# ScalarE's copy of turned tile 3 placed between the two halves of tile 1's k eviction

## The chip, the cores and the metric

The kernel runs on 1 core of a Trainium2 chip. The metric is the device time of one execution in microseconds, the median of several runs. The clock granted to TensorE was 1.00 in the profiled execution.

## The reference

Input x is 2048 x 640 in bf16. Out comes x, plus a linear attention block on the layer-normed x, plus a routed block of which eight rows are changed.

```python
xn = _layernorm(x, axis=-1)
return x + _A_ref(xn, A_wqkv, A_wo) + _B_ref(xn, B_w_r, B_w_gate, B_w_up, B_w_down)
# A: 32 heads of 20; phi = where(t > 0, t + 1, exp(t)) + 1e-6
#    kv = sum_s phi(k) v ; z = sum_s phi(k) ; o = phi(q) kv / (phi(q) z) ; o @ wo
# B: r = xn @ w_r ; the 8 rows with the largest r go through silu(x w_gate) * (x w_up) @ w_down,
#    scaled by sigmoid(r), and are added to xn at their places
```

## The kernel before

The 2048 rows are 16 tiles of 128 rows. The order on each engine is the order in which the program is written (`tc.manual_schedule()`), and each engine works through its own queue in that order; waits between engines are set by the data and by the buffers.

For each tile t the first phase does this. VectorE takes the statistics of x (`stat`, L176 and L178). The reciprocal root comes from ScalarE for tiles 0 to 3 and 8 (`root_act`, L182 and L183) and from GpSimd for the others (`root_pool`, L187 and L188). VectorE then writes the normed tile `xn` (`norm_dve`, L197). The tile must be turned, with its 640 features on the partitions, to be a weight for k = xn @ wk. Tiles 0 to 3 are turned on TensorE (`tr_pe`, L216: five 128 x 128 pieces, three into PSUM bank 7 and two into bank 6) and copied to `xnT` by `tr_ev`: the three pieces of bank 7 by ScalarE (L222) and the two of bank 6 by VectorE (L227). Tiles 4 to 15 are turned by a DMA on the SP queue (`tr_dma`, L230). On the same queue the load of x tiles 10 to 15 (`load_x`, L99) stands behind the transposes of tiles 4, 5 and 6, and weight loads stand between the later transposes.

k of a tile is two halves of 320 columns (`k_half`, L238, five matmuls each), in two PSUM banks: 2 and 3 for tile 1, 4 and 5 for tile 2, 0 and 1 for the others. The second half of each tile but tile 0 has a 321st column, the router's r. ScalarE evicts each half with an Exp and a Relu (`k_act`, L255 and L256), and copies the router column out of the second half (L258). VectorE joins both halves into phi(k) in one instruction (`k_phi`, L262). phi(k) and `xn` give the sum over rows that later makes kv (`g1`, L269, in banks 2 to 6). q is computed transposed, 20 pieces of 128 x 512 (`q_mm` L277, `q_act` L286 and L287, `q_phi` L293), the first three in the stretch around the change.

Around the change the program order, L413 to L447, is: first half of tile 0's eviction, statistics of tile 3, k of tile 1 with the turning of tile 2 between its halves, `tr_ev(2)`, the root of tile 3, the second half of tile 0's eviction, the router column of tile 0, **tile 1's eviction (both halves)**, statistics of tile 4 and norm of tile 3, k of tile 2 with the turning of tile 3 between its halves, **`tr_ev(3)`**, tile 2's eviction, and k of tile 3, which reads turned tile 3. The second phase, after tile 15's k, finishes the sums, the routed rows, the rest of q, and the output (`o_mm`, L833; `o_out`, L842).

Of the kernel before, what the change touches and what calls it, by code (L numbers as in the profile page):

```python
# [38 lines left out]
def kernel(  # L39
# [116 lines left out]
    def router_0():  # L156
        for kc in range(KC):
            PE.matmul(
                ps[:, 6, 400:401], lhsT=xnT[:, kc, 0:P], rhs=wk[:, kc, D : D + 1],
                start=(kc == 0), stop=(kc == KC - 1),  # L160
            )
# [13 lines left out]
    def stat(t, b):  # L175
        V.bn_stats(out=stats[:, t, b, :], in_=x_sb[:, t, b * HW : (b + 1) * HW])  # L176
        if b:
            V.bn_aggr(out=mv[:, t, :], in_=stats[:, t, :, :])  # L178
# [41 lines left out]
    def tr_ev(t, other=A):  # L220
        dst = xnT[:, :, t * P : (t + 1) * P]
        A.copy(dst[:, 0:3, :], psb[:, 7, 0 : 3 * P].rearrange("p (k f) -> p k f", k=3))  # L222
        src = psb[:, 6, 0 : 2 * P].rearrange("p (k f) -> p k f", k=2)
        if other is A:
            A.copy(dst[:, 3:, :], src)
        else:
            V.tensor_copy(dst[:, 3:, :], src)  # L227
# [6 lines left out]
    def k_half(t, b):  # L234
        b0 = K_BANK.get(t, 0)
        n = HW + (b if t else 0)
        for kc in range(KC):
            PE.matmul(  # L238
                ps[:, b0 + b, 0:n],
                lhsT=xnT[:, kc, t * P : (t + 1) * P],  # L240
                rhs=wk[:, kc, b * HW : b * HW + n],
                start=(kc == 0), stop=(kc == KC - 1),
            )
# [3 lines left out]
    def k_act(t, halves=(0, 1)):  # L247
        b0 = K_BANK.get(t, 0)
        if t not in kev:
            e = evk.tile([P, 2, HW], BF16, tag="ek", name=f"ek{t}")  # L250
            r = evk.tile([P, 2, HW], BF16, tag="rk", name=f"rk{t}")
            kev[t] = e, r
        e, r = kev[t]
        for b in halves:
            A.activation(e[:, b, :], ps[:, b0 + b, 0:HW], AF.Exp)  # L255
            A.activation(r[:, b, :], ps[:, b0 + b, 0:HW], AF.Relu)  # L256
            if b and t:
                A.copy(r_all[:, t : t + 1], ps[:, b0 + 1, HW : HW + 1])  # L258
# [163 lines left out]
    root_act(3)  # L422
    k_act(0, (1,))
    router_0()
    k_act(1)
    stat(4, 0)
    norm_dve(3)
    stat(4, 1)
# [2 lines left out]
    tr_pe(3)  # L431
    k_half(2, 1)
    tr_ev(3, V)
    k_act(2)
    stat(5, 0)
    k_phi(0)
# [499 lines left out]
```

## Time and profile before

| | us |
|---|---|
| median of 3 runs | 111.95 (111.92 to 112.37) |
| the profiled execution's own time | 112.4 |
| its span, first to last instruction | 110.7 |
| busy: TensorE, VectorE, ScalarE, GpSimd | 105.0, 83.2, 62.0, 41.0 |
| TensorE's wait for turned tile 3 at 13.14 | 0.78 |
| TensorE's wait for turned tile 15 at 50.37 | 0.16 |

Times in the trace are microseconds from the span's start. A row of a timeline has the start, the duration, the engine (PE is TensorE, PEld its weight loads, DVE VectorE, ACT ScalarE, POOL GpSimd, SPq the queue of DMAs that SyncE issues), the line of the kernel, the operation, the output and the inputs, and in brackets how long the engine stood idle before it and what released it. The chain of waits follows the last instruction back to what it hung on, and is printed in order of time. The table of stretches has, for each stretch, its length, the busy time and number of instructions of TensorE, its weight loads, VectorE, ScalarE and GpSimd, the granted clock, the busy share of the DMA engines and GB/s. Ends of matmuls are modelled, so a block's listed end may lie a little past the start of the next one.

### The profile page before, as it was taken

The page shows a single profiled execution, that of the slowest core. Times are in us where ns is not written, and L with a number is a line of the kernel's source. Part 1 is how long each engine was busy: PE and PEld are TensorE (multiplying, and loading weights), DVE is VectorE, ACT ScalarE, POOL GpSimd, SP SyncE. Part 2 cuts the span into 40 slices and gives each one's busy share as a digit, 9 for nine tenths or more (in the row PEclk, how much of TensorE's full clock was granted, in tenths as well). Part 3 has the DMA queues.
Part 4 walks back from the last instruction along what each step waited for, and adds up shares of the span by engine and source line. Part 5 has one row for each costly group of instructions (what it writes and reads, how often), then busy time and mean ns, then how long its engine had stood idle before and what let it go on. Part 6 is the DMA issues. An engine that isn't in the chain of part 4 may idle for free.

```text
span 110.7 us, 2559 instructions
## 1 busy us (share of the span) xinstructions
PE 105.0 (95%) x926; PEld 61.4 (55%) x926; DVE 83.2 (75%) x186; ACT 62.0 (56%) x160; POOL 41.0 (37%) x88
## 2 busy tenths in 40 slices
PE   5989799999999999999999999999999999999990
PEld 2256454665555565554436879534447766666660
DVE  1789987877999998753919964698599664788880
ACT  1449996799776666665019445588985735000000
POOL 6930273120067755899999430000000410000310
PEclk9999999999999999999999999999999999999999
DMA  3999237791758799989999979729928195783333
GB/s 84 325 341 331 103 65 63 131 328 20 197 138 160 194 182 220 199 189 287 259 248 401 391 260 266 219 68 319 356 79 177 32 330 188 169 322 118 114 121 118
DMA packets 28551, 22.46 MB, mean 203 GB/s; under 512 B 11634, under 2 KB 27258, under 8 KB 28538
## 3 DMA queue, kind: packets, MB, share of 16 engines
q1 hardware_dynamic: 23664, 18.44, 60.8%
q10 hardware_dynamic: 4810, 3.85, 11.1%
q8 instruction: 7, 0.11, 0.5%
q14 instruction: 6, 0.05, 0.2%
q0 software_dynamic: 64, 0.01, 0.1%
HBM read 14.79 MB, written 5.43 MB: 183 GB/s over the span
## 4 chain that ended last, share of the span: by engine, by line
PE 54%; DVE 22%; DMA 11%; POOL 5%; ACT 3%; issue 2%; SPq 0%; POOLq 0%; ACTq 0%
PE ps L833 19%; PE ps L277 12%; DMA x_sb<-in_A_x_dram 8%; DVE pk L262 6%; DVE stats L176 5%; DVE xn L197 5%; PE ps L269 5%; PE ps L531 4%; DVE pqT L293 3%; DMA xnT<-xn 3%; PE ps L238 3%; POOL rs L188 2%; DVE mv L178 2%; PE ps L685 2%; PE ps L768 2%
## 5 line engine op out<-in xcount | busy, mean ns | idle before, releaser
L238 PE MATMUL ps<-wk,xnT 128*128 128x320 bf16 (+1 forms) x160 | 25.0, 300 | 1.1 <-ACT xnT L222 1.0
L277 PE MATMUL ps<-xnT,wq 128*128 128x512 bf16 x100 | 23.7, 379 | 0.0
L833 PE MATMUL ps<-late,pqT 128*128 128x320 bf16 x150 | 21.8, 300 | 0.1
L238 PEld LDWEIGHTS <-xnT 128*128 128x128 bf16 x160 | 15.1, 97 | 9.7 <-ACT xnT L222 1.6
L269 PE MATMUL ps<-pk,xn 128*128 128x512 bf16 x80 | 19.6, 379 | 0.0
L255 ACT ACTIVATE ek<-ps 128x320 bf16<-128x320 f32 x32 | 14.6, 457 | 8.4 <-PE ps L238 8.4
L833 PEld LDWEIGHTS <-pqT 128*128 128x128 bf16 x150 | 13.9, 98 | 7.2 <-DVE pqT L640 1.9
L176 DVE BATCH_NORM_STATS2 stats<-x_sb 128x6 f32<-128x320 bf16 x32 | 14.7, 474 | 3.3 <-DMA x_sb<-in_A_x_dram 3.3
L286 ACT ACTIVATE eq<-ps 128x512 bf16<-128x512 f32 x20 | 12.0, 598 | 8.9 <-PE ps L277 8.9
L293 DVE SCALAR_TENSOR_TENSOR pqT<-eq,rq 128x512 bf16<-128x512 bf16 x20 | 14.2, 710 | 3.3 <-ACT rq L287 3.1
L842 DVE TENSOR_TENSOR o<-ps,x_sb 128x640 bf16<-128x640 f32 x15 | 12.4, 824 | 5.4 <-PE ps L833 3.0
L262 DVE SCALAR_TENSOR_TENSOR pk<-ek,rk 128x640 bf16<-128x640 bf16 x16 | 13.1, 823 | 3.2 <-ACT rk L256 3.2
L277 PEld LDWEIGHTS <-wq 128*128 128x128 bf16 x100 | 9.4, 98 | 10.6 <-issue 0.7
L256 ACT ACTIVATE rk<-ps 128x320 bf16<-128x320 f32 x32 | 14.6, 457 | 0.0
L208 POOL TENSOR_SCALAR x_sb<-x_sb,rs,nm 128x640 bf16<-128x640 bf16 x13 | 13.9, 1079 | 0.6
L269 PEld LDWEIGHTS <-xn 128*128 128x128 bf16 x80 | 7.6, 98 | 8.1
L287 ACT ACTIVATE rq<-ps 128x512 bf16<-128x512 f32 x20 | 11.9, 593 | 0.0
L187 POOL TENSOR_SCALAR t<-mv 128x1 bf16<-128x1 f32 x11 | 3.6, 326 | 22.2 <-DVE mv L178 22.0
L197 DVE TENSOR_SCALAR xn<-x_sb,mv,rs 128x640 bf16<-128x640 bf16 x16 | 8.3, 516 | 3.1 <-POOL rs L188 2.4
L188 POOL TENSOR_TENSOR rs<-t,mhalf 128x1 f32<-128x1 bf16 x11 | 9.4, 858 | 0.9
L884 POOL DMA_INDIRECT s_dram<-y,idx_i x1 | 1.6, 1594 | 20.4 <-ACT y L880 20.4
L869 ACT CAST o<-ps 128x160 bf16<-128x160 f32 x1 | 0.3, 293 | 13.9 <-PE ps L859 13.9
(129 smaller groups left out, 104.2 us busy)
## 6 DMA issues: line engine op xcount, KB each, us to landing
wg<-in_B_w_gate_dram SPq DMA_DIRECT2D x5, 384.0 KB, 3.4
wu<-in_B_w_up_dram SPq DMA_DIRECT2D x5, 384.0 KB, 8.9
wd<-in_B_w_down_dram SPq DMA_DIRECT2D x4, 480.0 KB, 11.0
spare<-rd SPq DMA_DIRECT2D x3, 640.0 KB, 5.5
rd<-rden ACTq DMA_DIRECT2D x1, 1280.0 KB, 7.1
out_dram<-o SPq DMA_DIRECT2D x8, 160.0 KB, 2.3
out_dram<-o ACTq DMA_DIRECT2D x7, 160.0 KB, 2.6
wo<-in_A_wo_dram SPq DMA_DIRECT2D x2, 500.0 KB, 8.2
```

What stands on the lines that cost most here:

```text
L176: V.bn_stats(out=stats[:, t, b, :], in_=x_sb[:, t, b * HW : (b + 1) * HW])
L197: V.tensor_scalar(out=xn[:, t, :], in0=x_sb[:, t, :], scalar1=mv[:, t, 0:1], scalar2=rs[:, t : t + 1], op0=ALU.subtract, op1=ALU.mult,)
L208: G.tensor_scalar(out=x_sb[:, t, :], in0=x_sb[:, t, :], scalar1=rs1[:, sl], scalar2=nm[:, sl], op0=ALU.mult, op1=ALU.add,)
L238: PE.matmul(ps[:, b0 + b, 0:n], lhsT=xnT[:, kc, t * P : (t + 1) * P], rhs=wk[:, kc, b * HW : b * HW + n], start=(kc == 0), stop=(kc == KC ...
L255: A.activation(e[:, b, :], ps[:, b0 + b, 0:HW], AF.Exp)
L256: A.activation(r[:, b, :], ps[:, b0 + b, 0:HW], AF.Relu)
L262: V.scalar_tensor_tensor(out=pk[:, t, :].rearrange("p (b f) -> p b f", b=2), in0=e[:], scalar=1.0, in1=r[:], op0=ALU.min, op1=ALU.add,)
L269: PE.matmul(ps[:, 2 + c, :], lhsT=xn[:, t, c * P : (c + 1) * P], rhs=pk[:, t, 0:512], start=(t == 0), stop=(t == T - 1),)
L277: PE.matmul(ps[:, bank, :], lhsT=wq[:, kc, m * P : (m + 1) * P], rhs=xnT[:, kc, tb * 512 : (tb + 1) * 512], start=(kc == 0), stop=(kc == K ...
L293: V.scalar_tensor_tensor(out=pqT[:, m, tb * 512 : (tb + 1) * 512], in0=e[:], scalar=1.0, in1=r[:], op0=ALU.min, op1=ALU.add,)
L833: PE.matmul(ps[:, b0 + b, 0:HW], lhsT=pqT[:, kc, t * P : (t + 1) * P], rhs=Ms[:, kc, b * HW : (b + 1) * HW], start=(kc == 0), stop=(kc == ...
L842: V.tensor_tensor(out=o_t[:], in0=ps[:, b0 : b0 + 2, 0:HW], in1=x_sb[:, t, :].rearrange("p (b f) -> p b f", b=2), op=ALU.add,)
```

## The change

`k_act` takes the halves that it is to evict. Before, tile 1's eviction is one call with both. Now the first half stays where it was, and the second half stands behind `tr_ev(3)`.

```diff
     k_act(0, (1,))
     router_0()
-    k_act(1)
+    k_act(1, (0,))
     stat(4, 0)
     norm_dve(3)
     stat(4, 1)
...
     tr_pe(3)
     k_half(2, 1)
     tr_ev(3, V)
+    k_act(1, (1,))
     k_act(2)
     stat(5, 0)
     k_phi(0)
```

The one place where instructions move is ScalarE's queue between tile 0's eviction and tile 2's. `ek1` and `rk1` are the Exp and the Relu of tile 1, `ek2` and `rk2` those of tile 2, `ps` is PSUM, `xnT` the turned tiles; rows of before alone have a -, rows of the changed kernel alone a +.

```order
 L255 ACTIVATE ek1_259<-ps_72 128x320
 L256 ACTIVATE rk1_260<-ps_72 128x320
-L255 ACTIVATE ek1_259<-ps_72 128x320 [waits PE_49]
+L222 COPY xnT_80<-ps_72 128x3x128 [waits PE_49]
+L255 ACTIVATE ek1_259<-ps_72 128x320
 L256 ACTIVATE rk1_260<-ps_72 128x320
 L258 CAST r_all_129<-ps_72 128x1
-L222 COPY xnT_80<-ps_72 128x3x128 [waits PE_49]
 L255 ACTIVATE ek2_289<-ps_72 128x320
 L256 ACTIVATE rk2_290<-ps_72 128x320
```

The copy has moved ahead of three instructions. It keeps its wait for TensorE, which now stands ahead of the second Exp, and since the transposes of tile 3 lie behind the second half of tile 1's k on TensorE, the Exp needs no wait of its own any more. All other rows of ScalarE stand as before, and so do all rows of TensorE, VectorE, GpSimd and SP.

The SP queue's rows of which the prediction speaks are these, the same in both kernels: the transposes of tiles 4, 5 and 6, the load of x tiles 10 to 15, and the transposes of tiles 7 and 8.

```order
L230 DMA_TRANSPOSE xnT<-xn 128x5x128 [waits DMAHW4_49,DVE_49]
L230 DMA_TRANSPOSE xnT<-xn 128x5x128 [waits DMAHW5_49,DVE_49]
L230 DMA_TRANSPOSE xnT<-xn 128x5x128 [waits DMAHW6_49,DVE_49]
L99 DMA x_sb<-in_A_x_dram 128x6x640 [waits DMAHW7_49]
L230 DMA_TRANSPOSE xnT<-xn 128x5x128 [waits DMAHW0_49,DVE_49]
L230 DMA_TRANSPOSE xnT<-xn 128x5x128 [waits DMAHW1_49,DVE_49]
```

Nothing moved here: the load stands behind three transposes, each of which waits for VectorE's norm of its tile.

## The prediction

> **What bounds the kernel now.** First the head of the page, to see which engine is full.
>
> ```profile
> span 110.7 us, 2559 instructions
> PE 105.0 (95%) x926; PEld 61.4 (55%) x926; DVE 83.2 (75%) x186; ACT 62.0 (56%) x160; POOL 41.0 (37%) x88
> ```
>
> TensorE is busy for 95% of the span, so time can only come out of its 5.7 us of idle time or out of its work, and the change leaves the work alone. The question is which of its waits the change touches, and whether the end follows. Second, therefore, TensorE's timeline around the moved copy and at tile 15's k (start, duration, then idle time and its releaser in brackets).
>
> ```profile
> 11.23 0.45 PE L216 MATMUL ps<-ident,xn 128*128 128x128 bf16 x5
> 11.52 0.85 PE L238 MATMUL ps<-wk,xnT 128*128 128x321 bf16 x5
> 13.14 1.54 PE L238 MATMUL ps<-wk,xnT 128*128 128x320 bf16 x10 [0.78 <-ACT xnT L222]
> ...
> 15.60 1.24 PE L269 MATMUL ps<-pk,xn 128*128 128x512 bf16 x5
> ```
> ```profile
> 42.72 1.53 PE L238 MATMUL ps<-wk,xnT 128*128 128x320 bf16 x10
> ...
> 47.60 1.53 PE L238 MATMUL ps<-wk,xnT 128*128 128x320 bf16 x10
> ...
> 50.37 1.54 PE L238 MATMUL ps<-wk,xnT 128*128 128x320 bf16 x10 [0.16 <-DMA xnT<-xn]
> ```
>
> TensorE turns tile 3 from 11.23 (L216), does tile 2's second k half until 12.37, then stands 0.78 us until ScalarE has copied turned tile 3 (L222). From there it shows no idle note in its rows up to tile 15's k at 50.37, where it stands 0.16 us for a **DMA**: turned tile 15. So two paths meet at 50.37. TensorE's own would have been there at 50.37 - 0.16 = 50.21; the transposed tile landed later.
>
> Third, the chain of waits, which shows what that tile hung on.
>
> ```profile
> 16.80 0.45 DVE xn L197
> ...
> 18.98 0.40 SPq L230
> ...
> 19.43 6.15 DMA x_sb<-in_A_x_dram
> ...
> 46.55 0.45 DVE xn L197
> ...
> 47.02 3.30 DMA xnT<-xn
> 50.33 0.05 issue
> 50.37 1.54 PE ps L238 x10
> ```
>
> This chain passes the tiles' statistics, shifts and roots on VectorE and GpSimd, the load of x tiles 10 to 15 (from 19.43, for 6.15 us), VectorE again, and the transpose of tile 15 (47.02 to 50.33). I call it **the tile chain**. The 0.78 us wait of TensorE isn't on it. Fourth, the busy time of one stretch shows that the tile chain has no slack of its own behind the load.
>
> ```profile
> 25.60:43.30 17.70, 17.70 (x104) 9.92 (x103) 17.53 (x41) 12.64 (x37) 8.32 (x14) 1.00 0.70 163
> ```
>
> The columns are TensorE, its weight loads, VectorE, ScalarE and GpSimd. From the load's end to 43.3 VectorE is busy for 17.53 of 17.70 us and ScalarE for 12.64: VectorE works off a backlog here and waits for no ScalarE result. TensorE is without a gap there as well, which is why the two paths run side by side up to 50.
>
> **The change, part by part.** No instruction is added or taken away. On ScalarE one copy changes places with the Exp, the Relu and the one-column cast of tile 1's second half:
>
> ```profile
> 11.55 0.45 ACT L256 ACTIVATE rk<-ps 128x320 bf16<-128x320 f32 x1
> 11.87 0.46 ACT L255 ACTIVATE ek<-ps 128x320 bf16<-128x320 f32 x1
> 12.19 0.47 ACT L256 ACTIVATE rk<-ps 128x320 bf16<-128x320 f32 x1
> 12.50 0.21 ACT L258 CAST r_all<-ps 128x1 bf16<-128x1 f32 x1
> 12.54 0.55 ACT L222 COPY xnT<-ps 128x384 bf16<-128x384 bf16 x1
> 12.91 0.52 ACT L255 ACTIVATE ek<-ps 128x320 bf16<-128x320 f32 x1
> ```
>
> 1. *The copy.* ScalarE starts one of these every 0.32 us and the cast takes 12.54 - 12.50 = 0.04. In the place of the second Exp, at 11.87, the copy starts 12.54 - 11.87 = **0.67 us earlier**. Its own wait, for the transposes of tile 3, doesn't hold it: all five are over at 11.23 + 0.45 = 11.68. It ends at 11.87 + 0.55 = 12.42, so TensorE, free at 11.52 + 0.85 = 12.37, starts tile 3's k at about 12.47 and not at 13.14. The idle 0.78 falls to about 0.11. VectorE's part of tile 3 doesn't take over as the late one: its copy (L227, in the rows below) is over at 12.01.
>
> The Trainium skill, "ScalarE: Activation LUTs", section "What ACT_TABLE_LOAD costs", gives an Exp of 320 columns 186 + 0.833 x 320 = 453 ns with an overlap of about 93, thus one start each 0.36 us. The durations agree (0.44 to 0.47), the distance of the starts does not (0.32). By the page the copy would gain 2 x 0.36 + 0.04 = 0.76 and not 0.67; the measurement decides.
>
> 2. *What is moved back.* Exp, Relu and cast of tile 1's second half start one copy slot later, 12.91 - 12.54 = 0.37 us, and their output is there at about 12.19 + 0.47 + 0.37 = 13.03. Its reader is VectorE's k of tile 1 (L262, below), at 15.52: 2.5 us of room. From 12.91 on ScalarE's order is as before, and so are its times, as it is back to back there. TensorE's g1 of tile 0, now at 15.60 - 0.67 = 14.93, overwrites the banks from which k of tiles 1 and 2 and the router column are read; the last of these reads, below, ends at 14.23 + 0.31 = 14.54. Cost: nothing, with 0.39 us in hand.
>
> ```profile
> 14.23 0.31 ACT L164 CAST r_all<-ps 128x1 bf16<-128x1 f32 x1
> ```
> ```profile
> 11.73 0.28 DVE L227 COPY xnT<-ps 128x256 bf16<-128x256 bf16 x1
> ...
> 15.52 0.82 DVE L262 SCALAR_TENSOR_TENSOR pk<-ek,rk 128x640 bf16<-128x640 bf16 x1
> ```
>
> 3. *What TensorE does with 0.67 us.* It is earlier by that much at every later tile, until a transposed tile isn't there. Tiles 12 and 14, at 42.72 and 47.60 before, would start at 42.05 and 46.93. Their transposes left at 38.87 and 44.33:
>
> ```profile
> 38.87 1.21 SPq L230 DMA_TRANSPOSE xnT<-xn  x1
> ...
> 44.33 1.21 SPq L230 DMA_TRANSPOSE xnT<-xn  x1
> ```
> ```profile
> DMA to landing us min/median/max: 2.6/2.9/3.6
> ```
>
> With the median of 2.9 us they land at 41.8 and 47.2. By tile 14 TensorE has caught up with the tile chain, and at tile 15 it stands until 50.33 whatever it did before. Wait there: 0.16 + 0.67 = 0.83 us, less what it waited at the tiles just before.
>
> 4. *Does the tile chain itself move?* No DMA, no VectorE and no GpSimd instruction changes place, and the transposes' queue is not touched. VectorE's reads of ScalarE's results before 47 have room (2.5 us for the nearest, in step 2). I take 0, bounded by 0 and, above, by the copies' overlap: VectorE's L227 now runs beside ScalarE's copy out of the neighbouring bank, at most some 0.01 us by the 0.29 that such a copy took at 9.96, beside one:
>
> ```profile
> 9.96 0.29 DVE L227 COPY xnT<-ps 128x256 bf16<-128x256 bf16 x1
> ```
>
> **Sum** against the profiled execution's 112.4 us (1.7 more than its span): 0.67 gained at 12.4, 0.67 given back by 50.33, nothing from there on, 112.4 again. The runs' median is 111.95, the profiled execution 0.45 above it, which I put to the execution and not to the kernel; the forecast is that median, with at most a crumb off: **111.9 us**.
>
> **Rivals.** *Faster: the tile chain is earlier in other executions.* Only 0.12 us (50.33 - 50.21) make it the later path in this one. It has one odd row, the second transpose issued, which took 2.43 us where the others took 1.2:
>
> ```profile
> 15.63 2.43 SPq L230 DMA_TRANSPOSE xnT<-xn  x1
> ```
>
> The third and the load of x stand behind it. Had it taken 1.2, the third could have left when its tile was ready (16.80 + 0.45 = 17.25) and the load at about 18.5 and not 19.43, and VectorE's stall behind that load is 1.45 us long:
>
> ```profile
> 25.60 0.49 DVE L176 BATCH_NORM_STATS2 stats<-x_sb 128x6 f32<-128x320 bf16 x1 [1.45 <-DMA x_sb<-in_A_x_dram]
> ```
>
> The tile chain would come 0.9 earlier, TensorE would be the bound at 50.21, and the change would give all of its 0.67: 111.95 - 0.67 = 111.3. For it speak that row, tile 15's 3.30 us against the median of 2.9, and the 0.45 us between the runs. Against it: whatever shifts the first loads shifts both paths alike. A part of it (0.1 to 0.5 us) is quite possible and stays within 0.5%. Chance of over 0.56 us: 0.22.
>
> *Slower: one more slow issue on the transposes' queue.* Place: the SP queue at 17 to 19.4, where the load of x tiles 10 to 15 stands behind three transposes. If TensorE's and ScalarE's shifted work makes the third take 2.43 as well, the load leaves 1.2 us later, VectorE's stall grows from 1.45 to 2.65, tile 15 lands at 51.5, and the end is 1.2 later: 113.1. It decides from a load 0.56 us late. Against it: only one of twelve issues was slow, and nothing names the change as its cause. Chance 0.07.
>
> *The change doesn't do what it says: the copy stands in the way.* If the transposes ended later than 11.87 by some w, ScalarE would stand for w with tile 1's second half behind the copy. That ScalarE does stand so is seen at 6.11:
>
> ```profile
> 6.11 0.48 ACT L222 COPY xnT<-ps 128x384 bf16<-128x384 bf16 x1 [1.20 <-PE ps L216]
> ```
>
> With w = 0.67 TensorE gains nothing (112.0, within 0.5%); VectorE, and the time, would suffer only from w = 2.5, the room of step 2, and be 0.56 slower from w = 3.1 (112.5 and up). The rows put the transposes 0.19 ahead. The Trainium skill, "PSUM — Partial Sum Buffer", section "Engine vs sequencer instructions", says that ScalarE's queue is strictly first in, first out, so nothing could pass the waiting copy; the row at 6.11 agrees. Chance of a slower time this way: 0.01.
>
> **How the numbers follow.** Forecast, absorbed wholly or but for under 0.56 us: 0.70. Faster: 0.22. Slower: 0.07 + 0.01 = 0.08. The bound of 0.5% is about what a measurement of this kernel can tell from no change. The range reaches down to the full gain with a little scatter, 111.2, and up to the highest run of before, 112.4, which leaves out the slow issue.
>
> **What would show it.** Right: tile 3's copy at about 11.9, the k behind it at about 12.5 with 0.1 idle, the load of x at 19.4 as before, and an idle of up to 0.8 us put down to the transposed tiles (L238 from 46 to 50.4), tile 15's k again near 50.4. Wrong: tile 15's k at 49.7 with little idle ahead of it (the faster rival), the load after 20 (the slower one), or ScalarE idle ahead of the copy (the third). My step that can fail first is step 4, that the tile chain in the timed runs stands where this one execution shows it.

## The result and the profile after

The changed kernel takes **111.45 us** (median of 10 runs, 111.06 to 112.45), the kernel before 111.99 us (10 runs, 111.92 to 112.52) in the same comparison: a ratio of 0.995, 95% interval 0.9926 to 0.9974, so 0.54 us or 0.5% faster. The forecast was 111.9 in a range of 111.2 to 112.4. The changed kernel was compared a second time, with other runs: 111.95 us (12 runs, 111.24 to 112.28) against 112.07 (23 runs), ratio 0.9985, interval 0.9965 to 1.0006. The single runs of the first comparison spread over 1.4 us, and the experiments below ask what moves them. Only one execution of each kernel and comparison has a trace; what the others did is not seen in rows. All profiles below show a granted clock of 0.998 to 1.00.

The head of the changed kernel's page (its profiled execution took 111.98 us):

```profile
span 110.3 us, 2550 instructions
PE 104.1 (94%) x917; PEld 61.0 (55%) x926; DVE 84.1 (76%) x186; ACT 62.0 (56%) x160; POOL 41.3 (37%) x88
```

The span is 0.4 us shorter. The nine instructions fewer are nine missing matmul records, so TensorE's busy time can't be compared with that of before. ScalarE's timeline of the changed kernel at the place of the change:

```profile
11.72 0.45 ACT L256 ACTIVATE rk<-ps 128x320 bf16<-128x320 f32 x1
12.03 0.50 ACT L222 COPY xnT<-ps 128x384 bf16<-128x384 bf16 x1
12.39 0.48 ACT L255 ACTIVATE ek<-ps 128x320 bf16<-128x320 f32 x1
12.72 0.48 ACT L256 ACTIVATE rk<-ps 128x320 bf16<-128x320 f32 x1
13.04 0.22 ACT L258 CAST r_all<-ps 128x1 bf16<-128x1 f32 x1
13.08 0.52 ACT L255 ACTIVATE ek<-ps 128x320 bf16<-128x320 f32 x1
...
16.26 0.82 ACT L287 ACTIVATE rq<-ps 128x512 bf16<-128x512 f32 x1
```

And TensorE's, from the turning of tile 3 on:

```profile
11.39 0.45 PE L216 MATMUL ps<-ident,xn 128*128 128x128 bf16 x5
11.68 2.45 PE L238 MATMUL ps<-wk,xnT 128*128 128x321 bf16 x15
14.18 1.02 PE L277 MATMUL ps<-xnT,wq 128*128 128x512 bf16 x4
15.05 1.24 PE L269 MATMUL ps<-pk,xn 128*128 128x512 bf16 x5
16.12 2.32 PE L277 MATMUL ps<-xnT,wq 128*128 128x512 bf16 x10
...
38.64 1.24 PE L269 MATMUL ps<-pk,xn 128*128 128x512 bf16 x5
39.90 1.54 PE L238 MATMUL ps<-wk,xnT 128*128 128x320 bf16 x10
...
46.16 1.24 PE L269 MATMUL ps<-pk,xn 128*128 128x512 bf16 x5
47.29 1.54 PE L238 MATMUL ps<-wk,xnT 128*128 128x320 bf16 x10
48.67 1.24 PE L269 MATMUL ps<-pk,xn 128*128 128x512 bf16 x5
49.95 1.54 PE L238 MATMUL ps<-wk,xnT 128*128 128x320 bf16 x10
```

This execution runs 0.16 us late already at the turning of tile 3 (11.39 and not 11.23), so distances count and not clock times. The copy starts 12.03 - 11.39 = 0.64 after the turning, where it was 12.54 - 11.23 = 1.31: 0.67 us earlier, to the digit of the forecast. The k of tile 2's second half and of tile 3 are now one row of 15 with no idle time noted. A stretch that begins at 12.55 shows where tile 3's k starts in it:

```profile
12.59 1.54 PE L238 MATMUL ps<-wk,xnT 128*128 128x320 bf16 x10
```

That is 12.59 - 11.39 = 1.20 us after the turning (1.19 to 1.20 in all profiles of the changed order), where it was 13.14 - 11.23 = 1.91. **TensorE gains 0.71 to 0.72 us at the copy.** It still waits for the copy: ten matmuls of this block take 1.38 us to the next block's start (47.29 to 48.67), five 0.69, so that tile 2's half is done at 11.68 + 0.69 = 12.37, and tile 3's k stands another 0.22 us. By the same reckoning it stood 13.14 - (11.52 + 0.69) = 0.93 us before.

It then gives some back. A g1 block of five matmuls takes 1.07 to 1.08 us to the next block's start where nothing is late (here 15.05 to 16.12). From 38.64 the next k should start at 39.72 and starts at 39.90; from 46.16 at 47.24, and starts at 47.29; from 48.67 at 49.75, and starts at 49.95. That is 0.18 + 0.05 + 0.20 = 0.43 us. Modelled ends hide such waits: the profile notes no idle time there. In the profile of before it noted 0.16 us at tile 15, and the g1 block ahead of it is this:

```profile
48.97 1.24 PE L269 MATMUL ps<-pk,xn 128*128 128x512 bf16 x5
```

By the distance (48.97 + 1.08 = 50.05, start at 50.37) 0.32 us were lost there. The waits of the weight loads tell what was late, in the changed kernel from 10 to 52 us (waiting engine and line, releaser, us in total, times, longest):

```profile
DVE stats L176 <- DMA x_sb<-in_A_x_dram: 1.2, 1, 1.2
...
PEld L238 <- DMA xnT<-xn: 1.7, 4, 0.5
```

The tile chain in this execution, by the SP queue and by VectorE's stall for the load (the changed kernel's timelines):

```profile
15.79 2.53 SPq L230 DMA_TRANSPOSE xnT<-xn  x1
```
```profile
19.70 0.58 SPq L99 DMA_DIRECT2D x_sb<-in_A_x_dram  x1
```
```profile
25.57 0.49 DVE L176 BATCH_NORM_STATS2 stats<-x_sb 128x6 f32<-128x320 bf16 x1 [1.25 <-DMA x_sb<-in_A_x_dram]
```

The second transpose issued was slow again (2.53 us), the load left at 19.70, and VectorE's stall ended at 25.57, where it ended at 25.60 before. From there VectorE is as full as it was (17.53 of 17.70 us, the third column of the stretch):

```profile
25.60:43.30 17.70, 17.63 (x102) 9.86 (x102) 17.53 (x41) 12.15 (x36) 8.36 (x14) 1.00 0.70 160
```

So up to the transposes the tile chain stood where it had stood, and turned tile 15 left at 46.98 where it had left at 47.02. What differed is how long it took to land. These are tile 15's transpose before and in the changed kernel:

```profile
DMA to landing us min/median/max: 3.3/3.3/3.3
```
```profile
DMA to landing us min/median/max: 2.9/2.9/2.9
```

Tile 15's k therefore started at 49.95 and not at 50.37: 0.42 us earlier by the clock, and 0.42 + 0.16 = 0.58 us earlier counted from the turning. Of the 0.72 us gained, the waits took only 0.43 - 0.32 = 0.11 to 0.14 us more than they had taken before, although the load was as late.

### The profile page after: what moved, and what is told of

It reads as the page before. It is cut to its first block, busy times and chain, and to the rows that moved or that the text cites. A ratio compares the mean times of both kernels' runs of the same rounds, so it can differ in the third digit from the quotient of the medians.

```text
span 110.3 us, 2550 instructions
## 1 busy us (share of the span) xinstructions
PE 104.1 (94%) x917; PEld 61.0 (55%) x926; DVE 84.1 (76%) x186; ACT 62.0 (56%) x160; POOL 41.3 (37%) x88
## 3 DMA queue, kind: packets, MB, share of 16 engines
q1 hardware_dynamic: 23664, 18.44, 60.6%
## 4 chain that ended last, share of the span: by engine, by line
PE 88%; ACT 4%; DVE 2%; DMA 2%; issue 1%; ACTq 0%
PE ps L277 20%; PE ps L834 19%; PE ps L238 18%; PE ps L269 16%; PE ps L532 4%; DMA x_sb<-in_A_x_dram 2%; PE ps L686 2%; PE ps L769 2%; PE ps L669 1%; PE ps L860 1%; ACT xnT L222 1%; PE ps L600 1%; DVE stats L176 1%; PE ps L698 1%; PE ps L779 1%
## 5 line engine op out<-in xcount | busy, mean ns | idle before, releaser
L277 PE MATMUL ps<-xnT,wq 128*128 128x512 bf16 x93 | 22.9, 379 | 0.6 <-issue 0.3
L262 DVE SCALAR_TENSOR_TENSOR pk<-ek,rk 128x640 bf16<-128x640 bf16 x16 | 13.7, 862 | 2.6 <-ACT rk L256 2.6
```

What stands on the lines that cost most here:

```text
L262: V.scalar_tensor_tensor(out=pk[:, t, :].rearrange("p (b f) -> p b f", b=2), in0=e[:], scalar=1.0, in1=r[:], op0=ALU.min, op1=ALU.add,)
L277: PE.matmul(ps[:, bank, :], lhsT=wq[:, kc, m * P : (m + 1) * P], rhs=xnT[:, kc, tb * 512 : (tb + 1) * 512], start=(kc == 0), stop=(kc == K ...
```

## The experiments

The theory of the forecast, called A: tile 15's k starts when the later of two things is ready, TensorE or the transposed tile; the change moves the first by 0.7 us and the second not at all. Rival B: the waits at the transposed tiles cost nothing, and TensorE's queue alone decides.

**1 and 2: the load of x tiles 10 to 15 later, without and with the change.**

```diff
     tr_dma(6)
-    load_x(10, 16)
...
     tr_dma(7)
+    load_x(10, 16)
```

> The kernel before, with the load of x tiles 10 to 15 behind the transpose of tile 7, so that it leaves about 1.9 us later (21.6 and not 19.4 to 19.7). Theory A: VectorE's stall grows from 1.4 to about 3.3 us, transposed tile 15 lands at about 52.2, TensorE waits for it by some 2 us, and the time rises by 1.8 us to about 113.8. Rival B: 112.0.

> The changed kernel with the same late load. Theory A: transposed tile 15 lands when it does without the change, so the change is worth nothing here: about 113.8, the same as the kernel before with the late load within 0.2 us, with its wait at tile 15 larger by the 0.55 to 0.67 us gained at the copy. Rival B: 111.45, the change's gain of 0.54 stays.

Measured: 113.35 us without the change (ratio to the kernel before 1.0107, interval 1.0072 to 1.0142) and 113.58 with it (1.0125, 1.0092 to 1.0158). The change is worth nothing here, and the two intervals overlap. TensorE's timeline of the kernel before with the late load, and of the changed kernel with it:

```profile
37.82 1.53 PE L238 MATMUL ps<-wk,xnT 128*128 128x320 bf16 x10
41.35 1.54 PE L238 MATMUL ps<-wk,xnT 128*128 128x320 bf16 x10 [0.92 <-DMA xnT<-xn]
```
```profile
37.24 1.53 PE L238 MATMUL ps<-wk,xnT 128*128 128x320 bf16 x10
41.33 1.54 PE L238 MATMUL ps<-wk,xnT 128*128 128x320 bf16 x10 [1.48 <-DMA xnT<-xn]
```

One is ahead of the other by 0.58 at 37.8, waits 0.56 longer for tile 11, and both go on from 41.35 and 41.33. (At tile 3's k it was ahead by 13.14 - 12.26 = 0.88; the other 0.30 went at tile 8, for which it alone waited.) This is absorption in its pure form, and rival B falls. The size was off: VectorE's stall grew to 2.6 and 2.7 us and not to 3.3, so the loss was 1.3 to 1.5 us and not 1.8, and most of the wait was at tile 11 and not 15.

**3 and 4: the whole load earlier.**

```diff
     tr_dma(4)
+    load_x(10, 16)
...
     tr_dma(6)
-    load_x(10, 16)
```

> The kernel before, with the load of x tiles 10 to 15 issued ahead of the transpose of tile 5 instead of behind that of tile 6; nothing else. Theory A (two paths meet: tile 15's k starts when the later of TensorE and the transposed tile is ready): VectorE's stall for the load goes, the tile chain comes about 1.2 us earlier, and TensorE alone is the bound. Tile 15's k starts at 50.05 (48.97 plus the 1.08 that the sums before it take) and not 50.37, so the time falls by 0.3 us, to about 111.7. Rival B (TensorE's own queue is the only bound and the tile chain never counts): 112.0, as the kernel before.

> The changed kernel with the same early load. Theory A: the changed kernel's waits for transposed tiles go (about 0.18, 0.05 and 0.20 us in its profile, at tiles 11, 14 and 15), so it is 0.4 us faster than the changed kernel, about 111.0; the change is then worth its whole 0.55 to 0.67 against the same kernel without it. Rival B: 111.45, as the changed kernel.

Both were missed: 112.92 us without the change (ratio 1.0075, interval 1.0048 to 1.0103), 112.87 with it (1.0053, 1.0029 to 1.0077), slower than the kernel before. TensorE's timeline, without and with the change:

```profile
12.98 1.54 PE L238 MATMUL ps<-wk,xnT 128*128 128x320 bf16 x10 [0.78 <-ACT xnT L222]
21.97 1.54 PE L238 MATMUL ps<-wk,xnT 128*128 128x321 bf16 x10 [0.69 <-DMA xnT<-xn]
```
```profile
22.02 1.54 PE L238 MATMUL ps<-wk,xnT 128*128 128x321 bf16 x10 [1.45 <-DMA xnT<-xn]
```

The 960 KB load ahead of tile 5's transpose made that transpose late (up to 6.5 us from issue to landing, 3.6 at most before), and the two paths met at tile 5 and not at tile 15. The change's gain is again in the wait, 1.45 against 0.69 us. After tile 5 neither loses anything: tile 15's k starts at 50.75 and 50.79. The miss is one of the edit, and A holds in it too; but it didn't yet show the change with the tile chain out of the way.

**5 and 6: only tile 10 loaded earlier, by a DMA of its own.**

```diff
     tr_dma(5)
+    load_x(10, 11)
...
     tr_dma(6)
-    load_x(10, 16)
+    load_x(11, 16)
```

> The kernel before, with x tile 10 loaded by a DMA of its own ahead of the transpose of tile 6 (160 KB) and tiles 11 to 15 where the whole load stood; the earlier try with the whole load ahead of tile 5's transpose only moved the wait to tile 5. Theory A: VectorE's stall for tile 10 (1.45 us) goes, the tile chain comes about 1 us earlier, no transposed tile is late, TensorE's own queue decides, and the kernel before gains the 0.32 us that tile 15 costs it: about 111.7. Rival B (TensorE's waits at the transposed tiles are no cost): 112.0.

> The changed kernel with the same split load. Theory A: no wait for a transposed tile is left, so the change is worth its whole gain at the copy, 0.55 to 0.67 us against the kernel before with the split load, and the time is about 111.0. Rival B: as the changed kernel, 111.45. If the transpose of tile 6, now behind the small load, is late at TensorE, the gain is eaten there, and the profile shows the wait at tile 6.

Measured: 112.24 us without the change (ratio 1.0021, interval 1.0012 to 1.003) and 111.66 with it (0.9965, 0.995 to 0.998). The difference, 0.58 us, is as expected; the level of both is some 0.6 us too high. In both profiles VectorE no longer stalls for the load, and no tile is late: from tile 3's to tile 15's k 49.91 - 13.00 = 36.91 us pass without the change, the distance that I take as free of waits from here on. About 0.25 us are lost behind it: from tile 15's k to the end of the span 110.5 - 49.91 = 60.6 us pass, and 60.3 in the kernels with the old number of DMAs. The part up to the last cast is the same (57.4 us); from the issue of the last output's DMA, at 107.65, to the end of the span 2.85 us pass, where it was 110.7 - 108.13 = 2.57. Both profiles with the split load show it, and none of the others does. Why one DMA more should do that wasn't tried. The rest of the miss lay in my baseline: I had counted from an execution of before in which tile 15 was late, and most runs of before (median 112.07) seem to hold no such wait to gain. Experiment 10 bears that out.

**7: both halves of tile 1's eviction behind the copy.**

```diff
-    k_act(1, (0,))
...
     tr_ev(3, V)
-    k_act(1, (1,))
+    k_act(1)
```

> The changed kernel with both halves of tile 1's eviction behind the copy of turned tile 3. By the step on the copy: the copy would find ScalarE free at about 11.4 but waits for the transposes until about 11.7, with all evictions behind it; TensorE is busy until 12.5 either way, so nothing is gained: 111.45. By the rival that the copy stands in the way: ScalarE's queue is about 0.3 us later, the banks for the sums of tile 0 come free at about 15.0, where TensorE wants them at 15.05, and up to 0.2 us are lost: 111.5 to 111.65. A gain of over 0.2 us would show that the copy was still late in the changed kernel.

Measured: 111.69 us, ratio 0.9986 (0.996 to 1.0012). Against the two medians of the changed kernel (111.45 and 111.95) that is no difference that can be told. The profile shows the price more clearly. ScalarE, and TensorE from the turning to the third q block:

```profile
11.61 0.48 ACT L222 COPY xnT<-ps 128x384 bf16<-128x384 bf16 x1 [0.26 <-PE ps L216]
```
```profile
11.23 0.45 PE L216 MATMUL ps<-ident,xn 128*128 128x128 bf16 x5
...
14.65 1.24 PE L269 MATMUL ps<-pk,xn 128*128 128x512 bf16 x5
15.73 1.24 PE L277 MATMUL ps<-xnT,wq 128*128 128x512 bf16 x5
17.34 1.24 PE L277 MATMUL ps<-xnT,wq 128*128 128x512 bf16 x5 [0.37 <-ACT rq L287]
```

The copy stands 0.26 us for the transposes with everything behind it. TensorE does gain by it, against what was expected, since it still waited for the copy in the changed kernel: the first g1 starts at 14.65, 3.42 us after the turning (11.23), and not 15.05 - 11.39 = 3.66. It then pays more at another place than I had named: the third q block goes to the bank that the first q was in, and has to wait until ScalarE has read it. It starts 17.34 - 15.73 = 1.61 us after the block before it and not 1.08, 0.53 late, so that from here on TensorE is some 0.3 us later than in the changed kernel. In the changed kernel that read ends at 16.26 + 0.82 = 17.08, and the third q block wants the bank one block after the second starts, at 16.12 + 1.08 = 17.20: only 0.12 us are in hand. Of the two places between the halves is the better one for TensorE; a place between the first half's Exp and Relu wasn't tried.

**8: TensorE made late again by 0.65 us in the changed kernel.**

```diff
     q_act(2)
+    warm(3, 1)
     k_half(4, 1)
```

> The changed kernel with three needless matmuls of 512 columns (0.216 us each, 0.65 together) on TensorE ahead of tile 4's k, so that TensorE gives back about what the copy gained. Theory A: the waits at transposed tiles (0.43 us in the changed kernel's profile) take up most of it, so tile 15's k starts only some 0.2 to 0.3 us later, about 50.2, and the time is 111.6 to 111.75. Rival B: the whole 0.65 is added, 112.1.

Measured: 112.02 us, ratio 0.9997 (0.9984 to 1.0009): 0.57 us more than the changed kernel's 111.45 and 0.07 more than its 111.95. The expectation was missed, towards B. The profile says why. In this execution the load left early and no tile was late; SP's queue and VectorE's stall:

```profile
18.77 0.58 SPq L99 DMA_DIRECT2D x_sb<-in_A_x_dram  x1
```
```profile
24.27 0.49 DVE L176 BATCH_NORM_STATS2 stats<-x_sb 128x6 f32<-128x320 bf16 x1 [0.25 <-DMA x_sb<-in_A_x_dram]
```

The slowest transpose issue took 1.58 us and not 2.4 to 2.5. With 0.65 us of needless matmuls tile 15's k starts at 49.83, and 36.91 + 0.65 after tile 3's (12.28): nothing is absorbed because nothing is late. So where the tile chain stands seems to be a property not of the kernel but of the **execution**. That was the second theory, A2, against B2: that the spread comes from the first loads alone.

**9, 10 and 11: the changed kernel again, and tile 10 in the early load.** The last two add tile 10 to the load of tiles 8 and 9, with as many DMAs as before.

```diff
-        load_x(8, 10)
+        load_x(8, 11)
...
     tr_dma(6)
-    load_x(10, 16)
+    load_x(11, 16)
```

> The changed kernel once more, for a second profile and more runs beside the two below. Theory A2 (TensorE's gain at the copy is always there, and the arrival of the transposed tiles differs from execution to execution, with the issue of the second transpose and the load behind it): median 111.3 to 111.6, lowest near 111.1, and the spread comes with the load of x tiles 10 to 15: where it leaves by 18.8 no tile is late, where it leaves at 19.7 up to 0.4 us are lost at tiles 11 to 15. Rival B2 (the spread is in the first loads alone): the profile shows no wait at tiles 11 to 15, whatever the load does.

> The kernel before, with x tile 10 added to the early load of tiles 8 and 9, and tiles 11 to 15 where 10 to 15 were loaded: as many DMAs as before, so that the last output's landing, which was some 0.25 us longer with the load split in two, should not grow. Theory A2: VectorE no longer stalls at tile 10, no transposed tile is late in any execution; TensorE's queue bounds the kernel before in most executions already, so only the late executions go: median 111.9 to 112.0. Rival: the larger early load delays wq or tile 3, 0.2 us or more slower.

> The changed kernel with the same load. Theory A2: its whole gain of 0.67 to 0.73 us at the copy comes out in every execution: median 111.1 to 111.3, 0.2 to 0.4 us under the changed kernel and 0.65 to 0.75 under the kernel before with this load. Rival B2: as the changed kernel, 111.45.

Measured: the changed kernel 111.95 us (above the 111.3 to 111.6 that was expected, lowest 111.24); the kernel before with the new load 112.03 (ratio 1.0012, interval 0.9986 to 1.0038); **the changed kernel with the new load 111.27** (6 runs, 111.19 to 111.34 but for one of 113.54 with a granted clock of 0.985; ratio 0.992, interval 0.9897 to 0.9943). The load alone gives nothing, the change alone 0.1 to 0.5 us, both together 0.8 us. In this comparison the early load takes 0.68 us off the changed kernel and 0.04 off the kernel before: this says that in most runs of the changed kernel late tiles had eaten the gain.

The changed kernel's second profile (109.5 us of span, 111.24 us) is the other kind of execution. SP's queue, VectorE's stall, and TensorE at tiles 14 and 15:

```profile
18.68 0.58 SPq L99 DMA_DIRECT2D x_sb<-in_A_x_dram  x1
```
```profile
24.52 0.49 DVE L176 BATCH_NORM_STATS2 stats<-x_sb 128x6 f32<-128x320 bf16 x1 [0.53 <-DMA x_sb<-in_A_x_dram]
```
```profile
46.72 1.53 PE L238 MATMUL ps<-wk,xnT 128*128 128x320 bf16 x10
49.20 1.54 PE L238 MATMUL ps<-wk,xnT 128*128 128x320 bf16 x10
```

The load left 1.0 us earlier than in the first profile, and tile 15's k starts at 49.20 with 0.03 us lost. Of the 1.0 us, 0.32 are first loads that came earlier (the first transpose left at 13.36 and not 13.68), and 0.70 the issues of the three transposes. The slow issue is here the third one, and shorter, after a second one of 1.20:

```profile
15.47 1.20 SPq L230 DMA_TRANSPOSE xnT<-xn  x1
```
```profile
17.11 1.51 SPq L230 DMA_TRANSPOSE xnT<-xn  x1
```

With tile 10 loaded early VectorE doesn't stall in either kernel, and TensorE, without and with the change:

```profile
13.01 1.54 PE L238 MATMUL ps<-wk,xnT 128*128 128x320 bf16 x10 [0.78 <-ACT xnT L222]
...
49.91 1.53 PE L238 MATMUL ps<-wk,xnT 128*128 128x320 bf16 x10
```
```profile
11.22 0.45 PE L216 MATMUL ps<-ident,xn 128*128 128x128 bf16 x5
...
49.31 1.53 PE L238 MATMUL ps<-wk,xnT 128*128 128x320 bf16 x10
```

**12: TensorE late by 0.65 us with the tile chain out of the way.** The edit of experiment 8 on the kernel of experiment 11.

> The changed kernel with x tile 10 in the early load, and three needless matmuls of 512 columns (0.65 us) on TensorE ahead of tile 4's k. Theory A2: with no transposed tile late, nothing takes up a delay of TensorE, so the whole 0.65 is added to the 111.27 of the kernel without them: 111.9, where the kernel before with the same load stands (112.03), as the three matmuls cost about what the copy gains. If some slack is left at the transposed tiles: 111.5 to 111.7.

Measured: 112.01 us, ratio 0.9996 (0.9979 to 1.0014), that is 0.74 more than without the three matmuls: the whole delay and 0.1 more. Between the two profiled executions the first loads make that 0.1 (turning at 11.32 and not 11.22). No slack is left, and three matmuls of 0.65 us together undo the change. The runs spread from 111.73 to 112.46 here, with no tile late in the profile.

The profiles side by side. The loss is the distance from tile 3's to tile 15's k less 36.91 (and less 0.65 where the three matmuls stand); tile 3's k in the changed order is taken 1.19 us after the turning. Experiment 7, where tile 3's k is earlier, is left out.

| kernel | turning of tile 3 | lost up to tile 15 | tile 15's k | span |
|---|---|---|---|---|
| before | 11.23 | 0.32 | 50.37 | 110.7 |
| changed, first profile | 11.39 | 0.46 | 49.95 | 110.3 |
| changed, second profile | 11.07 | 0.03 | 49.20 | 109.5 |
| changed, 3 matmuls | 11.09 | 0.0 | 49.83 | 110.1 |
| before, tile 10 early | 11.09 | 0.0 | 49.91 | 110.2 |
| changed, tile 10 early | 11.22 | 0.0 | 49.31 | 109.6 |
| changed, tile 10 early, 3 matmuls | 11.32 | 0.0 | 50.07 | 110.4 |
| before, late load | 11.23 | 1.21 | 51.26 | 111.6 |
| changed, late load | 11.07 | 2.07 | 51.24 | 111.6 |
| before, early load | 11.06 | 0.86 | 50.75 | 111.0 |
| changed, early load | 11.07 | 1.62 | 50.79 | 111.1 |
| before, split load | 11.09 | 0.0 | 49.91 | 110.5 |
| changed, split load | 11.63 | 0.0 | 49.73 | 110.3 |

From tile 15's k to the end of the span all of them take 60.3 to 60.4 us, but for the two with the split load, with 60.6. Beside the 0.72 us at the copy, the second and third columns therefore decide the time: the first loads shift the whole execution (by 0.3 us between the two profiles of the changed kernel, by 0.56 us with the split load), and the late tiles take from nothing to all of the gain. Between the two profiles of the changed kernel 0.32 us are the first loads and 0.43 the late tiles, so that neither A2 nor B2 holds alone for the spread of single runs. That late tiles matter is shown by experiments 10 and 11; how the spread of the timed runs divides between the two is not shown.

## Why the prediction was right or wrong, point by point

**The bound: two paths that meet at tile 15's k.** Right, and shown: with the late load both kernels continue from the same moment, and with tile 10 early TensorE alone decides. The size of the wait there was read too small. The 0.16 us of idle time noted was 0.32 us of loss, because a block's listed end lies past the point at which the next could start: TensorE's own path would have been there at 50.05, not at 50.21, and the tile was later than it by about 0.3 and not 0.12 us.

**Step 1, the copy.** Right: 0.67 us earlier. For TensorE it was worth 0.72 (1.91 to 1.19 us from the turning to tile 3's k) and not 0.67: in its new place the copy takes 0.50 us and not 0.55, and tile 3's k starts some 0.05 us after the copy's end in both. The idle time that is left is 0.22 us by the distances, where the forecast had 0.11. The 0.36 us between two starts that the prediction works out from the Trainium skill, "ScalarE: Activation LUTs", section "What ACT_TABLE_LOAD costs", is again not what the trace shows: the moved instructions start 0.32 to 0.33 us apart (12.39, 12.72, 13.04).

**Step 2, what is moved back.** Right in its result, nothing was lost, but the nearest margin was not the one that I named. I found 0.39 us ahead of g1's banks; q's bank had 0.12. Experiment 7 went past it and lost 0.53 us there.

**Step 3, TensorE is earlier until a tile is not there.** Right: in the first profile after it lost 0.18 us at tile 11, then at 14 and 15. Tile 11 is not one that the forecast had named: its transpose left at 35.67, as before (35.71), but took 4.2 us to land, where the longest in the profile of before took 3.6.

**Step 4, the tile chain itself, and the term built on it.** Up to the issue of the transposes the first profile after bears out that the chain doesn't move: VectorE's stall ended at 25.57 and at 25.60 before, with a slow second transpose in both. What failed is the term of the sum, "0.67 given back by 50.33". In that very profile tile 15's k started at 49.95, and not again near 50.4, which the prediction names as the sign of being right: turned tile 15 landed in 2.9 us and not in 3.3. So 0.11 to 0.14 of 0.72 us were given back. In the second profile, at 49.20, nothing was. I took the one profiled execution's tile chain for the kernel's, and it differs from execution to execution, in where the load leaves and in how long a transpose takes to land. The load of x left at 18.68 to 19.70 in the profiles with the load in its old place, and VectorE stalled 0.25 to 1.45 us for it; the profiled execution of before was the one with the longest stall of them, and at 112.4 us near the top of the kernel's runs. By the medians 0.54 us of the 0.72 came out in the first comparison, and 0.12 in the second. So the mechanism, that late tiles take up TensorE's gain, was right, and its size was taken from one execution. It is partly luck that the time fits: 111.45 lies within the range because the range reached down to the faster rival's full gain, and the sum by itself gives no gain at all.

**The rivals.** The faster one had the mechanism: the second transpose issued takes 2.15 to 2.70 us in six of the 14 profiles and 1.2 to 1.3 in the others, and the load behind it carries that on to the later tiles. It left out that in the others the third issue is the slow one, with 1.5 to 2.2 us, so that the load left at 18.7 to 19.2 and not at 18.5. It named the full gain, 111.3 us, for executions in which the second issue is short; the changed kernel's profiled execution of that kind took 111.24 us, and its six lowest runs of the first comparison, which have no trace, lie at 111.06 to 111.54. The true median lies between my forecast and this rival, and I had said that a gain of 0.1 to 0.5 us in between was quite possible; it should have been the forecast, since the evidence for it (a slow issue once in twelve, the profiled execution 0.45 us above the median) was quoted beside it. The slower rival didn't occur: no profile shows a second slow issue on top. The copy standing in the way didn't occur in the changed kernel, and did in experiment 7 with 0.26 us.

What stays open: why one transpose's issue takes 1.5 to 2.7 us, and why one tile lands in 2.9 us and another in 4.2; no run tried to change either. Also open is how often the tile chain is late. The two comparisons of the changed kernel have the same code and medians 0.5 us apart, and no trace says what differed between them. And it is not shown that the change leaves the slow issue alone: the second issue was the slow one in four of the five profiles without the change and in two of the nine with it, which is too few to tell.

## What to carry to other kernels

Where two paths arrive within some tenths of a microsecond of each other, a gain on one is worth what the other leaves of it, and one profiled execution doesn't tell which is later in the others: look whether that execution is a typical one, and what in it is out of line. A cheap test is to move the second path on purpose: late, to see the gain vanish; out of the way, to see all of it. Here the change paid 0.1 to 0.5 us by itself and 0.8 us together with an early load of one tile, which by itself showed no gain (0.04 us).

## What the runs showed of the hardware that was not expected

- The issue of a DMA transpose on the SP queue took 1.2 to 1.3 us nearly always, and once in each profiled execution 1.5 to 2.7 us: the second one in six profiles (2.15 to 2.70), the third one in eight (1.51 to 2.19).
- A 960 KB load issued ahead of a transpose on the same queue made the transpose land up to 6.5 us after its issue, where 3.6 us was the longest in the profile of before.
- With one load split in two, 2.85 us and not 2.57 passed from the issue of the last output's DMA to the end of the span, at the other end of the kernel.
- Idle time noted for TensorE can be half of what a block loses: 0.16 us noted, 0.32 us by the distance of the starts. At tile 3's k in the changed kernel none was noted, and 0.22 us were lost.
